# Early loads, interleaved attention pieces and an early w3 fetch in a retention-and-two-FFN kernel

## The chip, the core and the metric

The kernel runs on one core of one Trainium2 chip. The metric is the time on the device in microseconds (us); the median over several executions counts. One more execution was profiled: the trace has every instruction of the five engines, PE (TensorE matmul), DVE (VectorE), ACT (ScalarE), POOL (GpSimd) and SP (SyncE), and every DMA.

## The reference

Three stages follow each other: a decayed linear attention, a feed-forward layer with a piecewise quadratic activation, and a bilinear feed-forward layer with two output matrices.

```python
# attention: B, H, S, D = 4, 8, 768, 64
for t in range(S):
    state = gamma * state + k[:, :, t] (outer) v[:, :, t]
    y[:, :, t] = scale * q[:, :, t] @ state
x = y as (3072, 512)
# first layer: w_in (512, 2048), w_out (2048, 512)
h = x @ w_in
g = where(h >= 1, h, where(h <= -1, 0, (h + 1)**2 / 4))
x = g @ w_out
# second layer: w1, w2 (512, 1024), w3 (1024, 1024), w_out2 (1024, 512)
out = ((x @ w1) * (x @ w2) @ w3) @ w_out2
```

The weights arrive as 64-bit numbers and are turned into 32-bit floats on the chip.

## The kernel before, in words

The 3072 tokens are 6 tiles of 512. The attention runs over chunks of 128 tokens, so a tile is four chunks (g = 0 to 3 for the first). A chunk is three pieces (number a = 3g + part). Part 0 (L348, called qk here) multiplies the chunk's k and q into a PSUM tile `pa`; DVE multiplies that by the causal mask into `a_t` (L391). Part 1 (L358, called kv) multiplies k and v into `pa`; DVE makes `sbd` (chunk 0, L403) or `state` (L406) of it. Part 2 (L372, called out) multiplies the scaled q with `sbd` (not in chunk 0), then `a_t` with v, into `pa`; ACT copies it to `xh` (L412), DVE makes the next `sbd` of `state` (L415) and the remainder `xl` (L417). `piece_mm` issues a piece's matmuls, `piece_ew` what follows on ACT and DVE. `pa` has one buffer. Before the matmuls DVE or POOL multiplies q by `decay` (L315) and POOL scales v (L316).

For the first tile the loop is plainly: matmuls of piece a, loads and scaling for later chunks (`chunk_ahead`), elementwise work of piece a. q has two buffers, v and k one each. All loads are issued by SP, in the order of the code.

The conversion of weights is a generator of DVE steps (L184 to L215 or L231: five or six instructions on 512 or 1024 columns) that a small planner, `dve()`, fits into the gaps it expects on DVE. The first unit, win 0 and win 1 (the first two 128-column blocks of w_in), is converted one by one; then come pairs: wo 0 and 1 (of w_out), win 2 and 3, wo 2 and 3, and so on. A converted win block is split into a high part on ACT (L98) and a remainder on DVE (L99). The main loop then emits, for each step n, the matmuls `hps` of block f (L102 to L104: 12 matmuls, three per 128 rows), the activation `r` (L461 to L463) and the matmuls `y1acc` with w_out. Pieces of the later tiles lie between them.

All of w3, w1, w2 and w_out2 is converted in the same way during the first tiles and written to DRAM (`spill`). In the last tile (f = 0 to 15 counts its steps) w1 and w2 are fetched again and combined (`fetch_ab`, `prepare_ab`), and w_out2 is fetched and split (`load_wo2`). Then comes a stage that multiplies w3 by w_out2 (the w3 stage): 16 steps u, each with 12 matmuls of 128x512 into `w3acc`. Step u splits block u + 1 (`load_w3`, ACT then DVE) and then fetches block u + 2 into one of two buffers of tag f. The last two `prepare_ab`, the fetches of y (`fetch_y1`), their sums (`add_y`) and splits (`split_y`) and the evacuation of the product to `wc` lie in the same stage.

Of the kernel before, what the change touches and what calls it, by code (L numbers as in the profile page):

```python
# [37 lines left out]
PLAIN = 11  # L38
SINGLE = 1
# [10 lines left out]
def retention_then_two_ffns(  # L50
# [260 lines left out]
    def scale_chunk(g):  # L311
        if g >= NG:
# [4 lines left out]
            out=vp[g % 2],  # L317
# [16 lines left out]
    def piece_mm(a):  # L334
# [4 lines left out]
        q_t, kb, vb = ch[g], kp[g % 2], vp[g % 2]  # L339
        if part == 1 and c == NCH - 1:  # L340
            return
        ps = ps_a.tile([P, 2, 512], F32, tag="pa", name="pa")
        if part == 0:

            for p in range(NP):
                for h in range(2):
                    r = slice(64 * h, 64 * h + 64)
                    nc.tensor.matmul(  # L348
                        out=ps[:, h, p * C:(p + 1) * C], lhsT=kb[r, p, :], rhs=q_t[r, p, :],
                        start=True, stop=True,  # L350
                    )
            pe(1.0, ready[("q", g)])
        elif part == 1:

            for p in range(NP):
# [8 lines left out]
        else:  # L364


            for own in (False, True) if c else (True,):
                for j in range(NP // 2):
                    for h in range(2):
                        for e in range(2):  # L370
# [3 lines left out]
                                lhsT=vb[:, 2 * p + h, :] if own else sbd[r, p, :],  # L374
# [7 lines left out]
    def piece_ew(a):  # L382
# [6 lines left out]
        if part == 0:  # L389
            a_t = att.tile([P, 2, NP, C], F32, tag="a", name="a_t", bufs=1)  # L390
# [28 lines left out]
    def chunk_ahead(a):  # L419

        g, part = divmod(a, PIECES)
        if a < TILE_PIECES:
            if part == 0:
                if g:
                    load_qk(g + 1)
                scale_chunk(g + 1)
            elif part == 1:
                load_k(g + 1)
                load_v(g + 2)
        elif part == 0:  # L430
# [304 lines left out]
    with tc.manual_schedule():  # L735
# [14 lines left out]
        nc.sync.dma_start(out=decay, in_=c_decay)  # L750
        load_qk(0)
        load_v(0)
        nc.sync.dma_start(out=small, in_=c_small)
        scale_chunk(0)
        load_k(0)
# [4 lines left out]
        now["dma"] = 9.0  # L760
        load_job(jobs[0])
        load_v(1)


        early = [jobs[1]]
        for a in range(TILE_PIECES):
            piece_mm(a)
            chunk_ahead(a)
            if a == 2:
                load_job(early.pop(0))  # L770
            piece_ew(a)
# [4 lines left out]
        for n in range(-1, NA):  # L776
# [223 lines left out]
```

## Time and profile before

| what | value |
|---|---|
| median of 3 runs | 1108.78 us (1108.28 to 1109.03) |
| profiled execution, its own time | 1105.77 us |
| its span in the trace | 1104.0 us |
| PE busy | 1050.3 us, 95% of the span |
| DVE, ACT, POOL busy | 63%, 39%, 6% |

Engines run their own instructions in order and wait for each other by semaphores. PE is busy 95% of the span, so time can only come out of the other 5%, or out of matmuls that run at a lower clock: the granted clock of TensorE stands in a column of the stages, 1.00 for 2.4 GHz.

### The profile page before, as it was taken

What the parts mean: (1) busy time and instruction counts of PE and PEld (TensorE: products, weight loads), DVE (VectorE), ACT (ScalarE), POOL (GpSimd) and SP (SyncE); (2) the same over time, 40 slices, a digit from 0 to 9 for tenths busy, and PEclk for the clock granted to TensorE, in tenths of its full rate; (3) what the DMA queues carried; (4) which work ended last, traced back from release to release, by engine and by line L of the source; (5) the groups of instructions that cost most, each with busy time, mean ns of one, the idle gap of its engine ahead of it and who ended that gap; (6) DMA issues with size and microseconds to landing.
All of it is one profiled execution on the core that took longest, in us unless ns stands there. A gap on an engine that the chain in (4) does not pass through costs nothing.

```text
span 1104.0 us, 14147 instructions
## 1 busy us (share of the span) xinstructions
PE 1050.3 (95%) x5444; PEld 828.7 (75%) x5444; DVE 698.7 (63%) x1130; ACT 433.9 (39%) x763; POOL 71.5 (6%) x67
## 2 busy tenths in 40 slices
PE   4789999899999999999999998689999999999998
PEld 3555578677777777777788886478888888888886
DVE  4798888688888878877835774553445334623340
ACT  1223355344444445454435664432333223412220
POOL 2212000011110100000000010000000000000000
PEclk9789999999999999999999999899999999999999
DMA  6545225254443544354303665554544345523412
GB/s 208 181 154 181 77 96 183 85 172 173 164 152 124 170 136 153 124 173 142 115 2 132 248 239 196 185 200 172 187 166 143 131 176 172 189 105 134 167 34 77
DMA packets 64116, 166.03 MB, mean 150 GB/s; under 512 B 7600, under 2 KB 15920, under 8 KB 59312
## 3 DMA queue, kind: packets, MB, share of 16 engines
q1 hardware_dynamic: 61744, 150.44, 40.1%
q0 software_dynamic: 2304, 14.68, 3.7%
q8 instruction: 43, 0.70, 0.2%
q14 instruction: 25, 0.20, 0.1%
HBM read 125.24 MB, written 39.85 MB: 150 GB/s over the span
## 4 chain that ended last, share of the span: by engine, by line
PE 84%; DVE 6%; DMA 5%; ACT 2%; SPq 1%; issue 1%; POOL 1%; ACTq 0%; POOLq 0%; DVEq 0%
PE bank_a L673 12%; PE hps L103 8%; PE y1acc L102 8%; PE hps L102 8%; PE hps L104 8%; PE y1acc L103 7%; PE y1acc L104 7%; PE bank_b L673 6%; PE oacc L718 4%; PE oacc L720 4%; PE oacc L719 4%; PE bank_c L673 3%; PE pa L372 3%; DMA f<-sp_w 2%; PE y1acc L513 2%; PE pa L348 2%
## 5 line engine op out<-in xcount | busy, mean ns | idle before, releaser
L102 PE MATMUL hps<-xh,win 128*128 128x512 f32 x384 | 154.7, 403 | 6.3 <-ACT win L98 5.0
L103 PE MATMUL hps<-xh,win 128*128 128x512 f32 x384 | 151.7, 395 | 0.5 <-DVE win L99 0.5
L104 PE MATMUL hps<-xl,win 128*128 128x512 f32 x384 | 150.8, 393 | 0.4 <-DVE xl L417 0.4
L673 PE MATMUL bank_a<-yop,unit 128*128 128x512 f32 x576 | 145.7, 389 | 0.0
L102 PE MATMUL y1acc<-gh,wo_s 128*128 128x512 f32 x340 | 139.0, 409 | 4.9 <-ACT wo_s L98 4.9
L461 ACT ACTIVATE r<-hps 128x512 f32<-128x512 f32 x96 | 57.3, 597 | 218.3 <-PE hps L104 218.3
L103 PE MATMUL y1acc<-gh,wo_s 128*128 128x512 f32 x340 | 134.2, 395 | 0.5 <-DVE wo_s L99 0.5
L104 PE MATMUL y1acc<-gl,wo_s 128*128 128x512 f32 x340 | 133.6, 393 | 0.0
L463 DVE SCALAR_TENSOR_TENSOR r<-hps,r 128x512 f32<-128x512 f32 x96 | 66.3, 691 | 101.2 <-ACT r L462 100.7
L673 PEld LDWEIGHTS bank_a<-yop,unit 128*128 128x128 f32 x576 | 108.1, 188 | 22.5
L699 DVE TENSOR_TENSOR c<-bank_b,c 128x512 f32<-128x512 f32 x24 | 16.6, 692 | 131.5 <-PE bank_b L673 131.5
L102 PEld LDWEIGHTS hps<-xh,win 128*128 128x128 f32 x384 | 72.6, 189 | 25.2 <-ACT win L98 5.7
L103 PEld LDWEIGHTS hps<-xh,win 128*128 128x128 f32 x384 | 72.6, 189 | 18.6 <-DVE win L99 1.6
L104 PEld LDWEIGHTS hps<-xl,win 128*128 128x128 f32 x384 | 72.7, 189 | 17.0 <-DVE xl L417 1.3
L102 PEld LDWEIGHTS y1acc<-gh,wo_s 128*128 128x128 f32 x340 | 64.1, 189 | 23.7 <-ACT wo_s L98 5.7
L104 PEld LDWEIGHTS y1acc<-gl,wo_s 128*128 128x128 f32 x340 | 64.1, 189 | 14.5
L103 PEld LDWEIGHTS y1acc<-gh,wo_s 128*128 128x128 f32 x340 | 64.2, 189 | 13.9 <-DVE wo_s L99 1.6
L474 ACT CAST gh<-r 128x512 fp32r<-128x512 f32 x85 | 52.9, 622 | 52.6 <-DVE r L463 52.6
L673 PE MATMUL bank_b<-yop,unit 128*128 128x512 f32 x288 | 73.1, 389 | 0.0
L475 DVE TENSOR_TENSOR gl<-r,gh 128x512 fp32r<-128x512 f32 x85 | 60.6, 713 | 14.9 <-ACT gh L474 13.8
L99 DVE TENSOR_TENSOR wo_s<-wo_f,wo_s 128x512 fp32r<-128x512 f32 x85 | 61.9, 728 | 1.9 <-ACT wo_s L98 1.9
L315 POOL TENSOR_TENSOR q_t<-q_t,decay 128x512 f32<-128x512 f32 x23 | 32.6, 1416 | 465.4 <-DMA q_t<-in_qT_dram 438.0
(152 smaller groups left out, 1716.6 us busy)
## 6 DMA issues: line engine op xcount, KB each, us to landing
unit<-wab_d SPq DMA_DIRECT2D x24, 1024.0 KB, 4.8
unit<-wab_d SPq DMA_DIRECT2D x24, 768.0 KB, 4.3
raw<-in_w_in_dram SPq DMA_DIRECT2D x64, 128.0 KB, 3.0
raw<-in_w_dram SPq DMA_DIRECT2D x16, 512.0 KB, 4.0
raw<-in_w3t_dram SPq DMA_DIRECT2D x16, 512.0 KB, 3.8
wab_d<-four POOLq DMA_DIRECT2D x8, 1024.0 KB, 5.2
raw<-in_w_out_dram SPq DMA_DIRECT2D x14, 512.0 KB, 3.6
q_t<-in_qT_dram SPq DMA_DIRECT2D x24, 256.0 KB, 4.4
```

The lines of the kernel that those rows point to most:

```text
L99: nc.vector.tensor_tensor(out=lo, in0=src, in1=hi, op=ALU.subtract)
L102: nc.tensor.matmul(out=ps, lhsT=lh, rhs=rh, start=first, stop=False)
L103: nc.tensor.matmul(out=ps, lhsT=ll, rhs=rh, start=False, stop=False)
L104: nc.tensor.matmul(out=ps, lhsT=lh, rhs=rl, start=False, stop=last)
L461: nc.scalar.activation(out=r, in_=hps[n], func=AF.Relu, bias=0.5, scale=0.5)
L463: nc.vector.scalar_tensor_tensor(out=r, in0=hps.pop(n), scalar=1.0, in1=r, op0=ALU.max, op1=ALU.min)
L474: nc.scalar.copy(out=gh, in_=gs[n])
L475: nc.vector.tensor_tensor(out=gl, in0=gs[n], in1=gh, op=ALU.subtract)
L673: nc.tensor.matmul(out=ps, lhsT=x, rhs=z, start=first and kb + k == 0, stop=kb == 1 and k == 2, skip_group_check=True,)
L718: nc.tensor.matmul(out=ps, lhsT=lh, rhs=wh, start=(f == 0), stop=False)
L719: nc.tensor.matmul(out=ps, lhsT=lh, rhs=wl, start=False, stop=False)
L720: nc.tensor.matmul(out=ps, lhsT=ll, rhs=wh, start=False, stop=(f == NF2 - 1))
```

## The change

Five edits, in the parts that the diff shows. The first tile's four chunks get loads of their own, all issued at the start into buffers of the weight pool (`load_early`); POOL scales v in place. The constants and the loads of win 0 and win 1 are issued by ACT, not SP; each of the eight weight loads waits there until an earlier one of ACT's loads has landed. The pieces of the first tile run in a written order (`EARLY_ORDER`: number, 0 for matmuls and 1 for elementwise) with two `pa` buffers and, for part 1, the four buffers of `ps_acc`. The loads of chunk 4 and part of chunk 5 follow directly. `fetch_w3` loads w3 in pairs into the eight buffers that `wc` uses later, in steps f = 8 to 15 of the last tile.

```diff
+EARLY_ORDER = [(0, 0), (0, 1), (1, 0), (3, 0), (1, 1), (3, 1), (2, 0), (4, 0), (6, 0), (2, 1), (4, 1), (6, 1)]
+EARLY_ORDER += [(5, 0), (7, 0), (9, 0), (5, 1), (7, 1), (9, 1), (8, 0), (10, 0), (8, 1), (10, 1), (11, 0), (11, 1)]
...
-    ps_h = ctx.enter_context(tc.tile_pool(name="ps_h", bufs=2, space=bass.MemoryType.PSUM))
-    ps_a = tc.tile_pool(name="ps_a", bufs=1, space=bass.MemoryType.PSUM)
...
+    ps_a = early_psum.enter_context(
+        tc.tile_pool(name="ps_e", bufs=2, space=bass.MemoryType.PSUM)
+    )
...
+    first_keys = (("win", 0), ("win", 1))
...
+            queue = nc.scalar if key in first_keys else nc.sync
...
-        one = key[0] in ("wo2", "w3")
+        one = key[0] == "wo2"
...
+    def load_early():
+
+        for g in range(EARLY):
+            qk = wpool.tile([P, 2, 512], F32, tag="w", name="qk_e")
+            vk = wpool.tile([P, 2, 512], F32, tag="w", name="vk_e")
+            ch[g], kb[g] = (qk[:, i, :].rearrange("p (a t) -> p a t", a=NP) for i in range(2))
+            vt[g] = vb[g] = vk[:, 0, :].rearrange("p (h d) -> p h d", h=H)
+            kt[g] = vk[:, 1, :]
+            nc.sync.dma_start(out=ch[g], in_=qT[g])
+            nc.sync.dma_start(out=kb[g], in_=kT[g])
...
+            nc.sync.dma_start(out=vt[g], in_=v[g])
...
+            nc.sync.dma_start(out=kt[g], in_=k[g])
...
-        ps = ps_a.tile([P, 2, 512], F32, tag="pa", name="pa")
+        if g < EARLY and part == 1:
+            ps = ps_acc.tile([P, 1, 512], F32, tag="acc", name="pa")
+        else:
+            ps = ps_a.tile([P, 2, 512], F32, tag="pa", name="pa")
...
+            if g < EARLY:
+                a_t = wpool.tile([P, 2, 512], F32, tag="w", name="a_e")
...
+    def fetch_w3(u):
+
+        t = late.tile([P, 2, 512], F32, tag="wc", name="w3f", bufs=NF2)
+        for i in range(2):
+            nc.sync.dma_start(out=t[:, i, :], in_=spill[("w3", u + i)])
+            arrived[("w3", u + i)] = t[:, i, :]
...
+        nc.scalar.dma_start(out=decay, in_=c_decay)
+        nc.scalar.dma_start(out=small, in_=c_small)
         for h in range(2):
             r = slice(64 * h, 64 * h + 64)
-            nc.sync.dma_start(out=block[r], in_=c_block[r, :, 64 * h:64 * h + 64])
-        load_qk(1)
...
+            nc.scalar.dma_start(out=block[r], in_=c_block[r, :, 64 * h:64 * h + 64])
+        load_early()
         load_job(jobs[0])
...
+        load_job(jobs[1])
+        load_qk(EARLY)
+        load_v(EARLY)
+        load_k(EARLY)
+        for g in range(EARLY + 1):
+            scale_chunk(g)
+        load_v(EARLY + 1)
...
+        for a, ew in EARLY_ORDER:
+            (piece_ew if ew else piece_mm)(a)
+        early_psum.close()
...
-                    if j == NF2 - 1:
-                        fetch(("w3", 0), spill[("w3", 0)])
                 elif last:
                     load_wo2(NF2 - 1)
-                    fetch(("w3", 1), spill[("w3", 1)])
+                if f >= NF2:
+                    fetch_w3(2 * (f - NF2))
...
-            if u + 2 < 2 * NF2:
-                fetch(("w3", u + 2), spill[("w3", u + 2)])
```

PE, at the start of the program: before, the pieces of a chunk stand one behind the other (L348 is qk, L358 kv, L372 out).

```order
L348 MATMUL pa<-q_t,kp_90 128x128 x8
L358 MATMUL pa<-vp_92,k_t 64x64 x8
L372 MATMUL pa<-a_t,vp_92 64x128 x8
L348 MATMUL pa<-q_t,kp_91 128x128 x8
L358 MATMUL pa<-vp_93,k_t 64x64 x8
L372 MATMUL pa<-q_t,sbd 64x128 x8
L372 MATMUL pa<-a_t,vp_93 64x128 x8
L348 MATMUL pa<-q_t,kp_90 128x128 x8
```

After, qk of the next chunk and kv of this one stand ahead of each out piece (L380 is qk, L390 kv, L404 out; `qk_e` and `vk_e` are the new load buffers, `a_e` the masked product).

```order
L380 MATMUL pa<-qk_e 128x128 x8
L390 MATMUL pa<-vk_e 64x64 x8
L380 MATMUL pa<-qk_e 128x128 x8
L404 MATMUL pa<-a_e,vk_e 64x128 x8
L390 MATMUL pa<-vk_e 64x64 x8
L380 MATMUL pa<-qk_e 128x128 x8
L404 MATMUL pa<-qk_e,sbd 64x128 x8
L404 MATMUL pa<-a_e,vk_e 64x128 x8
```

The qk matmuls of chunk 1 moved ahead of the out matmuls of chunk 0, and those of chunk 2 ahead of the out matmuls of chunk 1.

DVE, in the same stretch, from the mask of chunk 1 on: before, the conversion of win 0 (`u`, `w_f`) begins behind the second `a_t`.

```order
L391 TENSOR_TENSOR a_t<-pa,small 128x1024
L184 TENSOR_SCALAR u<-u 128x512
L189 TENSOR_SCALAR u<-u 128x512
L194 SCALAR_TENSOR_TENSOR w_f<-raw,u 128x512
L406 TENSOR_TENSOR state<-pa,sbd 128x256
L199 TENSOR_SCALAR u<-w_f 128x512
L203 SCALAR_TENSOR_TENSOR u<-raw,u 128x512
L215 TENSOR_TENSOR w_f<-w_f,u 128x512
L415 TENSOR_TENSOR sbd<-state,block 128x256
L417 TENSOR_TENSOR xl<-pa,xh 128x4x128
```

After, the rows from the mask of chunk 3 (the last of the tile) to the `xl` of chunk 3.

```order
L427 TENSOR_TENSOR a_e<-pa,small 128x1024
L191 TENSOR_SCALAR u<-u 128x512
L196 TENSOR_SCALAR u<-u 128x512
L201 SCALAR_TENSOR_TENSOR w_f<-raw,u 128x512
L451 TENSOR_TENSOR sbd<-state,block 128x256
L453 TENSOR_TENSOR xl<-pa,xh 128x4x128
L442 TENSOR_TENSOR state<-pa,sbd 128x256
L206 TENSOR_SCALAR u<-w_f 128x512
L210 SCALAR_TENSOR_TENSOR u<-raw,u 128x512
L222 TENSOR_TENSOR w_f<-w_f,u 128x512
L451 TENSOR_TENSOR sbd<-state,block 128x256
L453 TENSOR_TENSOR xl<-pa,xh 128x4x128
```

All four masks now stand ahead of the first conversion instruction, so that when the tile's last `xl` is done (L453) only the conversion of win 0 is done, where before win 0, win 1 and four steps of wo 0 and 1 were.

SP, from the last tile into the w3 stage: before, the fetches of w3 (`sp_w_0` and on) begin around the writes of y (`y_d`) and then stand between the fetches of w1/w2 (`sp_wab`) and of y.

```order
L275 DMA f_5671<-sp_wo_6_2333 128x512
L275 DMA f_5748<-sp_wo_7_2386 128x512
L275 DMA f_5750<-sp_w_0_3634 128x512
L545 DMA y_d_86<-y1st 128x512 x4
L275 DMA f_5779<-sp_w_1_3696 128x512
L275 DMA f_5791<-sp_w_2_3755 128x512
L275 DMA f_5831<-sp_wab_3518 128x512
L275 DMA f_5833<-sp_wab_3569 128x512
L275 DMA f_5838<-sp_w_3_3812 128x512
L275 DMA f_5855<-sp_w_4_3920 128x512
L275 DMA f_5872<-sp_w_5_3987 128x512
```

After, they stand in pairs between the fetches of w_out2 (`sp_wo`) and w1/w2 of the last tile.

```order
L591 DMA w3f<-sp_w_0_3634 128x512
L591 DMA w3f<-sp_w_1_3696 128x512
L591 DMA w3f<-sp_w_2_3755 128x512
L591 DMA w3f<-sp_w_3_3812 128x512
L282 DMA f_5574<-sp_wo_5_2213 128x512
L282 DMA f_5576<-sp_wab_3349 128x512
L282 DMA f_5578<-sp_wab_3452 128x512
L591 DMA w3f<-sp_w_4_3920 128x512
L591 DMA w3f<-sp_w_5_3987 128x512
L591 DMA w3f<-sp_w_6_4039 128x512
L591 DMA w3f<-sp_w_7_4104 128x512
L282 DMA f_5683<-sp_wo_6_2333 128x512
```

The first w3 fetches moved from behind the last tile's last w_out2 fetch to ahead of the sixth, and their buffers (`w3f`) are not shared with it.

## Rows read from the trace of the kernel before

**Rows 1.** Waits of PE over the span: engine line, released by, us, times, longest

```profile
PE w3acc L102 <- ACT w3s L98: 10.9, 5, 5.0
PE pa L358 <- issue: 9.8, 5, 3.2
```

**Rows 2.** Stages: us, busy us by engine, PEclk, DMA share, GB/s

```profile
0.00:3.00 3.00, 0.00 (x0) 0.00 (x0) 0.00 (x0) 1.28 (x1) 0.20 (x4) 1.00 0.37 104
3.00:6.00 3.00, 0.81 (x8) 0.84 (x10) 0.69 (x1) 0.00 (x0) 0.00 (x0) 1.00 1.03 354
0.00:43.00 43.00, 22.07 (x241) 17.99 (x241) 21.97 (x34) 7.22 (x11) 10.03 (x13) 0.84 0.66 206
632.00:676.00 44.00, 41.45 (x182) 33.43 (x180) 30.91 (x63) 27.83 (x58) 3.19 (x6) 1.00 0.55 199
```

**Rows 3.** Timeline, first tile: start us, us, engine line operation [idle before <-releaser]

```profile
9.73 1.26 POOL L315 TENSOR_TENSOR q_t<-q_t,decay 128x512 f32<-128x512 f32 x1 [2.60 <-DMA q_t<-in_qT_dram]
...
13.70 2.08 PE L348 MATMUL pa<-q_t,kp 64*128 64x128 f32 x16 [1.46 <-issue]
15.82 1.23 DVE L391 TENSOR_TENSOR a_t<-pa,small 128x1024 f32<-128x1024 f32 x1 [2.22 <-PE pa L348]
16.96 0.42 DVE L184 TENSOR_SCALAR u<-u 128x512 f32<-128x512 f32 x1
...
18.48 0.42 DVE L406 TENSOR_TENSOR state<-pa,sbd 128x256 f32<-128x256 f32 x1
...
20.00 0.69 DVE L215 TENSOR_TENSOR w_f<-w_f,u 128x512 f32<-128x512 f32 x1
20.02 1.97 PE L372 MATMUL pa<-a_t,vp 128*64 128x128 f32 x16
...
22.66 0.69 DVE L417 TENSOR_TENSOR xl<-pa,xh 128x512 fp32r<-128x512 f32 x1 [1.63 <-ACT xh L412]
...
23.45 1.16 PE L348 MATMUL pa<-q_t,kp 64*128 64x128 f32 x16 [1.46 <-POOL vp L316]
...
42.98 0.50 PE L102 MATMUL hps<-xh,win 128*128 128x512 f32 x1 [0.69 <-ACT xh L412]
```

**Rows 4.** Timeline, DVE and PE where the main loop begins

```profile
58.13 1.29 DVE L99 TENSOR_TENSOR win<-w_f,win 128x512 fp32r<-128x512 f32 x2 [0.69 <-ACT win L98]
...
58.15 0.50 PE L102 MATMUL hps<-xh,win 128*128 128x512 f32 x1 [0.58 <-ACT win L98]
77.41 0.79 PE L102 MATMUL hps<-xh,win 128*128 128x512 f32 x1 [3.19 <-ACT win L98]
...
84.53 0.69 DVE L463 SCALAR_TENSOR_TENSOR r<-hps,r 128x512 f32<-128x512 f32 x1 [2.52 <-ACT r L462]
```

**Rows 5.** Tile w3acc: first and last start of its first line's matmuls

```profile
L102 PE MATMUL w3acc<-wo,w3s x64: 387/389/796, 676.0 to 739.0; 128*128 128x512 f32 x64
```

**Rows 6.** Timeline, PE in the w3 stage

```profile
704.93 0.80 PE L102 MATMUL w3acc<-wo,w3s 128*128 128x512 f32 x1 [5.04 <-ACT w3s L98]
...
710.52 0.63 PE L102 MATMUL w3acc<-wo,w3s 128*128 128x512 f32 x1
710.94 0.63 PE L103 MATMUL w3acc<-wo,w3s 128*128 128x512 f32 x1
...
711.88 0.40 PE L103 MATMUL w3acc<-wo,w3s 128*128 128x512 f32 x1
712.11 0.39 PE L104 MATMUL w3acc<-wo,w3s 128*128 128x512 f32 x1
```

**Rows 7.** Timeline, ACT and DVE in the w3 stage

```profile
704.26 0.62 ACT L98 CAST w3s<-f 128x512 fp32r<-128x512 f32 x1 [8.43 <-DMA f<-sp_w]
...
716.35 0.68 DVE L99 TENSOR_TENSOR w3s<-f,w3s 128x512 fp32r<-128x512 f32 x1
...
720.37 0.69 DVE L651 TENSOR_TENSOR t__6056<-f,f 128x512 f32<-128x512 f32 x1 [1.53 <-DMA f<-y_d]
...
722.31 0.68 DVE L99 TENSOR_TENSOR w3s<-f,w3s 128x512 fp32r<-128x512 f32 x1
```

More of the change, by code (lines that the diff above doesn't have):

```diff
@@ L72, in retention_then_two_ffns @@
     ps_acc = ctx.enter_context(tc.tile_pool(name="ps_acc", bufs=4, space=bass.MemoryType.PSUM))
-    ps_h = ctx.enter_context(tc.tile_pool(name="ps_h", bufs=2, space=bass.MemoryType.PSUM))
-    ps_a = tc.tile_pool(name="ps_a", bufs=1, space=bass.MemoryType.PSUM)
-    pairs_psum = ctx.enter_context(ExitStack())
-    ps_a = pairs_psum.enter_context(ps_a)
+    early_psum, pairs_psum = (ctx.enter_context(ExitStack()) for _ in range(2))
+    ps_a = early_psum.enter_context(
+        tc.tile_pool(name="ps_e", bufs=2, space=bass.MemoryType.PSUM)
+    )
+    ps_h = None
     dram = ctx.enter_context(tc.tile_pool(name="dram", bufs=1, space=bass.MemoryType.DRAM))
@@ L285, in retention_then_two_ffns @@
     at = {}
+    EARLY = TT // C
+    kb = {}
+    vb = {}
+    def load_early():
[7 more added lines that the diff above has]
+            nc.sync.dma_start(out=kb[g], in_=kT[g])
+            ready[("q", g)] = dma(256)
+            ready[("kT", g)] = dma(256)
+            nc.sync.dma_start(out=vt[g], in_=v[g])
+            ready[("v", g)] = dma(256)
+            nc.sync.dma_start(out=kt[g], in_=k[g])
+            ready[("k", g)] = dma(256)
     def load_qk(g):
@@ L289, in load_qk @@
             q_t = att.tile([P, NP, C], F32, tag="q", name="q_t")
-            kb = kp[g % 2]
+            kb[g] = kp[g % 2]
             nc.sync.dma_start(out=q_t, in_=qT[g])
-            nc.sync.dma_start(out=kb, in_=kT[g])
+            nc.sync.dma_start(out=kb[g], in_=kT[g])
             ch[g] = q_t
@@ L301, in load_v @@
             vt[g] = v_t
+            vb[g] = vp[g % 2]
             ready[("v", g)] = dma(256, now["pool"])
@@ L316, in scale_chunk @@
         nc.gpsimd.tensor_tensor(
-            out=vp[g % 2],
+            out=vb[g],
             in0=v_t,
@@ L348, in piece_mm @@
                     nc.tensor.matmul(
-                        out=ps[:, h, p * C:(p + 1) * C], lhsT=kb[r, p, :], rhs=q_t[r, p, :],
+                        out=ps[:, h, p * C:(p + 1) * C], lhsT=k_[r, p, :], rhs=q_t[r, p, :],
                         start=True, stop=True,
@@ L373, in piece_mm @@
                                 out=ps[64 * e:64 * e + 64, h, j * C:(j + 1) * C],
-                                lhsT=vb[:, 2 * p + h, :] if own else sbd[r, p, :],
+                                lhsT=v_[:, 2 * p + h, :] if own else sbd[r, p, :],
                                 rhs=at[g][:, h, p, :] if own else q_t[r, p, :],
@@ L389, in piece_ew @@
         if part == 0:
-            a_t = att.tile([P, 2, NP, C], F32, tag="a", name="a_t", bufs=1)
+            if g < EARLY:
+                a_t = wpool.tile([P, 2, 512], F32, tag="w", name="a_e")
+                a_t = a_t.rearrange("p h (a t) -> p h a t", a=NP)
+            else:
+                a_t = att.tile([P, 2, NP, C], F32, tag="a", name="a_t", bufs=1)
             nc.vector.tensor_tensor(
@@ L421, in chunk_ahead @@
         g, part = divmod(a, PIECES)
[L422 to L430, printed above, removed]
+        if part == 0:
             load_k(g)
@@ L748, in retention_then_two_ffns @@
                 (jobs if at_ < SINGLE else later).append(one)
[L750 to L755, printed above, removed]
+        nc.scalar.dma_start(out=decay, in_=c_decay)
+        nc.scalar.dma_start(out=small, in_=c_small)
         for h in range(2):
             r = slice(64 * h, 64 * h + 64)
-            nc.sync.dma_start(out=block[r], in_=c_block[r, :, 64 * h:64 * h + 64])
-        load_qk(1)
-        now["dma"] = 9.0
+            nc.scalar.dma_start(out=block[r], in_=c_block[r, :, 64 * h:64 * h + 64])
+        load_early()
         load_job(jobs[0])
[L762 to L771, printed above, removed]
+        load_job(jobs[1])
[8 more added lines that the diff above has]
+        early_psum.close()
+        ps_h = ctx.enter_context(tc.tile_pool(name="ps_h", bufs=2, space=bass.MemoryType.PSUM))
+        ps_a = pairs_psum.enter_context(
+            tc.tile_pool(name="ps_a", bufs=1, space=bass.MemoryType.PSUM)
+        )
         todo = deque(range(TILE_PIECES, NSTEP))
```

6 lines of the change are left out of this document (3 added, 3 removed).

## The prediction

> **What bounds the kernel now.** I looked first at who PE waits for over the whole span, because PE is busy 95% of it. Two waits lead [rows 1]: 10.9 us in the w3 stage, for the split of a w3 block on ACT, and 9.8 us in front of the kv pieces, where the trace names no engine (the one `pa` buffer has to be read first). They lie at the two ends that the change touches. The stages [rows 2] give the size of each. In the first 43 us PE is busy for 22.07 and DVE for 21.97: neither is the bound, they take turns. The first matmul of the main loop starts at 42.98 [rows 3]. The w3 stage, 676 to 740, is 192 matmuls long, and its waits and slow matmuls are taken apart below.
>
> Then I looked at what follows the first tile, since time won there must not be lost again. PE reaches win 2 at 58.15 and waits 0.58 us for it, reaches win 4 at 77.41 after 3.19 us of waiting [rows 4]. So from 43 to about 77 us the conversion on DVE is the bound, not PE. What the first tile gains counts only as far as DVE gets its conversions done earlier.
>
> **The first tile, step by step.** *Loads.* SP now issues 16 loads of 256 KB (4.19 MB), ACT the constants and win 0 and 1 (256 + 68 + 128 + 1024 KB, 1.51 MB). Before the change the DMA engines ran at a share of 1.03 and 354 GB/s from 3 to 6 us [rows 2], which is full. Up to 3 us they had moved 0.31 MB (3 us at 104 GB/s), 0.9 us of work at 354, so the first bytes flow at about 2.1 us. No row shows the short rows of win and block alone. Their cost lies between 354 GB/s and 206, the mean of the first tile [rows 2]; I take 206 for those 1.18 MB, since that is the only row that holds such loads, and 354 for the other 4.53 MB: 12.8 + 5.7 = 18.5 us, so the last load of chunk 3 lands at 20.6. All at 354 it would be 18.2; all at 206, 29.8.
>
> The rate of 354 came from SP alone. Weights issued by ACT therefore are not free, and I count them in the sum. The Trainium skill says the same in its page DMA: Bandwidth & Descriptors, section Issuing engines are not separate DMA queues: transfers of all issuers run on the same 16 engines, and a second issuer saves only the time to issue. By it the sum stays as it is; were the ACT loads free, chunk 3 would be there at 14.0 us, and the first tile would win 6.6 us more.
>
> *From chunk 3's loads to the main loop.* q of chunk 3 is issued three loads earlier, 2.2 us at 354, so it is there at 18.4, scaled by POOL at 19.7 (1.26), and qk is done at 20.9 (1.16 at the high clock). v lands one load ahead of k, at 19.9, and its scaling does not hold up qk. Then DVE runs a string in the new order [rows 3]: mask 1.23, three conversion steps 0.42 + 0.42 + 0.69, sbd 0.42, xl 0.69, state 0.42, three conversion steps 0.42 + 0.69 + 0.69, sbd 0.42, xl 0.69: 7.2 us, so 28.1. In between it waits for kv and two out pieces; such an out half took 1.97 us at the low clock. I add 2 us, the length of one of them: the main loop starts at **30** instead of 43. Were PE at the low clock all through (2.08 for a qk where 1.16 is the other level), it would be 5 us more. ACT issues twelve DMAs, the last eight each after an earlier one landed, ahead of its first copy (`xh` of chunk 0). As that copy is wanted after the second chunk's qk, I cost it at nothing; without that cover it holds up out of chunk 1 by some 2 us.
>
> *What DVE has not done by then.* In the new order DVE has done by that point one q (0.69), four masks (4.92), seven sbd or state (2.94), four xl (2.76) and six conversion steps (3.33): 14.6 us of work, against 21.97 [rows 2]. The missing 7.4 us, win 1 and the first steps of wo 0 and 1, come after. Before, win 2 came 15.2 us after the start of the loop (42.98 to 58.15); now 15.2 + 7.4 = 22.6 us after, at 52.6. So of 13 us 5.5 are left. PE then stands idle some 8 us more in that stretch, and comes back at a low clock: after the 3.19 us wait at 77.41 the first matmul took 0.79 and DVE then stood 2.52 us before the next r [rows 4]. I take 1.5 off (0 to 2.5). The first tile gives **4.0 us**. From win 2 on both orders are the same, and the waits at 77 us only move with DVE.
>
> **The w3 stage.** Its first line of matmuls starts at 676.0 and last at 739.0, with three pitches after it to the end [rows 5]: 63.7 us. A matmul at the high clock starts 0.23 us after the one before [rows 6], so 192 of them are 43.7 us. The excess is 20.0. Its largest wait, 5.04 us before 704.93 [rows 6], goes back to ACT standing 8.43 us until a w3 fetch landed [rows 7], and 14 matmuls behind it start 0.43 apart [rows 6], 2.9 us more. With w3 fetched from f = 8 on, no load of w3 is waited for, because the last pair is issued when the stage begins and is wanted 14 steps later. The buffers of `wc` are free then: step 7 evacuates into those of blocks 0 to 7, split by step 6.
>
> What stays: the start of the stage (0.5 us, and eight matmuls at the 0.43 pitch, 1.6 us), since nothing ahead of it moves. In steps 4 to 9 the splits stand on DVE behind `prepare_ab`, `add_y` and the evacuation; I allow 1.3 us in all. And one wait remains whole: `add_y` stands ahead of the split of block 10 and waits for a y load that is issued only when an earlier split frees its buffer. DVE's split of block 9 starts at 716.35, of block 10 at 722.31, with 1.53 us of waiting for y and four sums between [rows 7]; 6.0 us, for which PE has 12 matmuls, 2.7 us. 3.3 us remain, and with them perhaps 14 matmuls at the low clock, 0 to 2.9; I take 1.6. Sum 0.5 + 1.6 + 1.3 + 3.3 + 1.6 = 8.3, so the stage gives 20.0 - 8.3 = **11.7 us** (9 where DVE is later by 2.7, 14 where no low clock follows and the splits cost nothing).
>
> The fetches move 4.2 MB into the last tile. From 632 to 676 the DMA share was 0.55 at 199 GB/s [rows 2]; 4.2 MB in 44 us are 95 GB/s more, 294, below 354. I cost them at nothing.
>
> **Sum.** 4.0 + 11.7 = 15.7 us. The profiled execution took 1105.77 us (span 1104.0, 1.8 around it), so 1090.1. The median of the runs lies 3.0 us above it; on that scale it is 1093.
>
> **Rivals.** *DVE takes all of the first tile back.* If all loads run at 206 GB/s, chunk 3 is there at 29.8, the loop starts at 39 and win 2 comes at 61.8, 3.7 us later than before. With the w3 stage at its low end, 9 us, the gain is 5.3: 1103.5. For it speaks that the rate fell to 206 in the mean, against it that this mean contains stretches in which no load was asked for (share 0.66).
>
> *Both ends pay fully.* All loads at 354, or the weights of ACT free: loop start at 27, win 2 at 49.6, no clock loss, 8.5 us, and w3 14: 22.5, so 1086.3. For it speaks that PE is denser in the new order and may hold the high clock; against it the short rows of win.
>
> *The last tile starves (slower).* The w3 fetches stand on SP ahead of w1/w2 and w_out2 fetches. If DMA does not keep up, `prepare_ab` holds DVE, and with it the splits that PE needs next. It decides where each of the eight steps is 2.3 us later: 18 us, more than the gain. Against it: 294 GB/s wanted, 354 shown.
>
> *The change does not do what it says.* If PE in the w3 stage waited for buffers and not for loads, only 4 us are won: 1104.8. Against it ACT's releaser, a DMA [rows 7]. The first tile's pieces do interleave, by the order of PE.
>
> **How the numbers follow.** My forecast has 0.55 (1089 to 1101 by its own bounds: the first tile between -1.0 and 5.5, w3 between 9 and 14), both ends full 0.19, DVE takes it back 0.16, no effect on w3 0.05, starving 0.05. The range 1084 to 1104 holds the forecast, the full case and most of the third, and leaves out about 0.15. About 0.2% (2.2 us) is what a measurement of this kernel can tell from no change: faster 0.92 (all but starving and a corner of the third), same 0.04, slower 0.04.
>
> **What would show it.** In the new trace: the last load of chunk 3 near 20.6 us, the first `hps` matmul near 30, win 2 near 52.6 after a wait of PE for its split; a w3 stage near 52 us long, with no wait for a w3 fetch and one of about 3 us near its tenth step. I am wrong if the loop starts later than 35, if win 2 is not what PE waits for, or if a load of y or a clock at 1.2 GHz fills the w3 stage again.

## The result and the profile after

The changed kernel takes 1093.16 us in the median (1091.85 to 1093.40, 4 runs) against 1108.90 (1108.28 to 1109.59, 4 runs): a ratio of 0.9855, 95% interval 0.9838 to 0.9873, 15.7 us less. The profiled execution took 1093.40 us (span 1091.6), 12.4 us less than the profiled one of before; where the other 3.3 us are, the first experiment shows.

The timeline after, at the end of the first tile and in the main loop; it answers to [rows 3, 4].

```profile
20.37 1.26 POOL L344 TENSOR_TENSOR qk_e<-qk_e,decay 128x512 f32<-128x512 f32 x1 [1.72 <-DMA qk_e<-in_qT_dram]
22.74 1.04 POOL L345 TENSOR_TENSOR vk_e<-vk_e,small 128x512 f32<-128x512 f32 x1 [1.10 <-DMA vk_e<-in_v_dram]
22.90 1.23 DVE L427 TENSOR_TENSOR a_e<-pa,small 128x1024 f32<-128x1024 f32 x1 [1.84 <-PE pa L380]
24.07 1.52 POOL L344 TENSOR_TENSOR q_t<-q_t,decay 128x512 f32<-128x512 f32 x1 [0.29 <-DMA q_t<-in_qT_dram]
24.49 1.37 DVE L196 TENSOR_SCALAR u<-u 128x512 uint32<-128x512 uint32 x1
25.90 1.41 DVE L201 SCALAR_TENSOR_TENSOR w_f<-raw,u 128x512 uint32<-128x512 uint32 x1
27.24 0.41 DVE L451 TENSOR_TENSOR sbd<-state,block 128x256 f32<-128x256 f32 x1
...
31.78 0.76 PE L106 MATMUL hps<-xh,win 128*128 128x512 f32 x1 [1.50 <-DVE xl L453]
44.95 5.40 PE L541 MATMUL y1acc<-r,wo_f 128*128 128x512 f32 x8 [3.88 <-DVE wo_f L238]
55.16 0.50 PE L106 MATMUL hps<-xh,win 128*128 128x512 f32 x1 [3.19 <-ACT win L102]
```

The main loop starts at 31.78 instead of 42.98, 11.2 us earlier; win 2 comes at 55.16 instead of 58.15. The first tile still waits for loads: POOL stood 1.72 us for the q of chunk 3 and 1.10 us for its v. Between the last mask (22.90) and `sbd` two conversion steps take 1.37 and 1.41 us; the same two for the next block, at 32.60 and 33.06, take 0.43 and 0.69.

The stages after (us, busy us by engine, PEclk, DMA share, GB/s); they answer to [rows 2].

```profile
3.00:6.00 3.00, 0.96 (x8) 0.99 (x10) 0.69 (x1) 0.00 (x0) 0.00 (x0) 1.00 0.97 305
6.00:9.00 3.00, 2.13 (x28) 1.76 (x24) 1.23 (x1) 0.00 (x0) 1.04 (x1) 1.00 1.05 288
9.00:13.00 4.00, 2.34 (x21) 2.00 (x20) 0.53 (x2) 0.00 (x0) 2.30 (x2) 1.00 1.10 278
13.00:17.00 4.00, 2.62 (x38) 2.49 (x38) 1.47 (x2) 1.87 (x2) 1.26 (x1) 1.00 1.07 274
17.00:20.00 3.00, 2.84 (x62) 2.41 (x59) 2.23 (x4) 0.57 (x2) 1.04 (x1) 1.00 1.11 292
...
632.00:672.00 40.00, 37.78 (x164) 30.36 (x163) 26.93 (x55) 25.25 (x52) 3.19 (x6) 1.00 0.81 294
```

From 3 to 20 us the DMA engines are full (share about 1.0 to 1.1) and move 274 to 305 GB/s. The clock column needs care there: it reads 1.00 wherever the trace has no record of the clock, here up to 14.63 us (in [rows 2] up to 21.96). The same out matmuls of three chunks tell more:

```profile
12.78 1.97 PE L404 MATMUL pa<-a_e,vk_e 128*64 128x128 f32 x16
...
18.29 1.09 PE L404 MATMUL pa<-a_e,vk_e 128*64 128x128 f32 x16
...
28.30 1.97 PE L404 MATMUL pa<-a_e,vk_e 128*64 128x128 f32 x16
```

The second stands under a record of 2.4 GHz, the third under one of 1.2 GHz; by its length the first ran at 1.2 GHz too. In the last tile, with the fetches of w3, the DMA engines move 294 GB/s at a share of 0.81.

The tile `w3acc` after, which answers to [rows 5]:

```profile
L106 PE MATMUL w3acc<-wo,w3s x64: 387/389/632, 672.3 to 726.7; 128*128 128x512 f32 x64
```

The waits of PE over the span (us, times, longest), to [rows 1]:

```profile
PE w3acc L107 <- DVE w3s L103: 5.4, 5, 2.9
...
PE w3acc L106 <- ACT w3s L102: 1.7, 1, 1.7
```

And the timeline of the w3 stage, to [rows 6, 7]:

```profile
672.32 0.50 PE L106 MATMUL w3acc<-wo,w3s 128*128 128x512 f32 x1 [1.71 <-ACT w3s L102]
...
692.97 0.69 DVE L686 TENSOR_TENSOR t__5960<-f,f 128x512 f32<-128x512 f32 x1 [2.51 <-DMA f<-y_d]
...
696.26 0.50 PE L107 MATMUL w3acc<-wo,w3s 128*128 128x512 f32 x1 [1.65 <-DVE w3s L103]
...
705.58 0.69 DVE L686 TENSOR_TENSOR t__6058<-f,f 128x512 f32<-128x512 f32 x1 [1.57 <-DMA f<-y_d]
...
708.26 0.79 PE L107 MATMUL w3acc<-wo,w3s 128*128 128x512 f32 x1 [2.94 <-DVE w3s L103]
708.85 0.63 PE L108 MATMUL w3acc<-wo,w3s 128*128 128x512 f32 x1
709.28 0.63 PE L106 MATMUL w3acc<-wo,w3s 128*128 128x512 f32 x1
```

The stage is 55.0 us long (first to last of its 192 matmuls and one pitch), 63.8 before. No wait for a fetch of w3 is left. What is left is two waits, 1.65 and 2.94 us, behind DVE's sums, which wait for y loads, and 22 matmuls that start more than 0.36 us after the one before, at 1.2 GHz, 9 at the stage's start and 13 behind the second wait. Counted from 0, the two waits lie in steps 7 and 10.

### The profile page after: what moved, and what is told of

It reads as the page before. It is cut to its first block, busy times and chain, and to the rows that moved or that the text cites. A ratio compares the mean times of both kernels' runs of the same rounds, so it can differ in the third digit from the quotient of the medians.

```text
span 1091.6 us, 14117 instructions
## 1 busy us (share of the span) xinstructions
PE 1047.6 (96%) x5444; PEld 828.7 (76%) x5444; DVE 700.1 (64%) x1130; ACT 434.0 (40%) x763; POOL 70.3 (6%) x67
## 4 chain that ended last, share of the span: by engine, by line
PE 87%; DVE 6%; DMA 3%; ACT 2%; issue 1%; POOL 0%; DVEq 0%; ACTq 0%; SPq 0%
PE bank_a L708 12%; PE hps L107 8%; PE hps L106 8%; PE hps L108 8%; PE y1acc L106 8%; PE y1acc L107 7%; PE y1acc L108 7%; PE bank_b L708 6%; PE oacc L753 4%; PE oacc L755 4%; PE oacc L754 4%; PE bank_c L708 3%; PE pa L404 3%; PE y1acc L541 2%; PE pa L380 2%; DMA raw<-in_w_in_dram 1%
## 5 line engine op out<-in xcount | busy, mean ns | idle before, releaser
L503 DVE TENSOR_TENSOR gl<-r,gh 128x512 fp32r<-128x512 f32 x85 | 60.1, 707 | 14.9 <-ACT gh L502 13.8
L708 PEld LDWEIGHTS bank_b<-yop,unit 128*128 128x128 f32 x288 | 54.1, 188 | 11.2
```

Of the source, the lines that this page charges most:

```text
L503: nc.vector.tensor_tensor(out=gl, in0=gs[n], in1=gh, op=ALU.subtract)
L708: nc.tensor.matmul(out=ps, lhsT=x, rhs=z, start=first and kb + k == 0, stop=kb == 1 and k == 2, skip_group_check=True,)
```

## The experiments

Unless another base is named, each is the changed kernel with one edit. "Stage" is the w3 stage as counted above, "half-clock" the number of its matmuls that start 0.36 to 0.47 us after the one before, where 0.23 is the pitch at 2.4 GHz.

| kernel | median us (range, runs) | ratio to before, 95% | win 2 at | w3 stage from, long | half-clock |
|---|---|---|---|---|---|
| before again | 1108.33 (1105.1-1110.57, 10) | 0.9993 (0.998-1.0006) | 60.30 | 679.9, 63.1 | 18 |
| w3 only | 1097.29 (1096.53-1099.4, 4) | 0.9902 (0.9881-0.9924) | 59.93 | 679.3, 52.0 | 8 |
| first tile only | 1103.98 (1101.2-1108.0, 10) | 0.9964 (0.9947-0.9982) | 54.55 | 670.9, 63.8 | 20 |
| weights behind | 1088.03 (1087.7-1089.1, 4) | 0.9817 (0.9794-0.9841) | 51.17 | 668.3, 53.4 | 14 |
| weights between | 1092.04 (1091.6-1094.74, 4) | 0.9851 (0.9832-0.987) | 57.17 | 674.4, 53.8 | 17 |
| two issuers | 1089.01 (1088.02-1090.16, 4) | 0.9825 (0.9805-0.9845) | 51.94 | 670.0, 51.9 | 6 |
| POOL late | 1093.01 (1092.27-1093.71, 4) | 0.9861 (0.9845-0.9878) | 55.84 | 673.2, 53.3 | 14 |
| conversion early | 1092.66 (1088.37-1093.0, 4) | 0.9849 (0.9825-0.9873) | 55.69 | 673.7, 53.2 | 13 |
| y early | 1090.69 (1086.66-1092.47, 4) | 0.9835 (0.981-0.9861) | 57.24 | 676.2, 49.0 | 0 |
| y order | 1090.38 (1089.9-1091.31, 4) | 0.9835 (0.9818-0.9852) | 57.27 | 674.7, 50.6 | 8 |
| both | 1084.25 (1083.29-1086.47, 4) | 0.9781 (0.9762-0.9801) | 51.45 | 668.8, 48.9 | 8 |
| both, sums later | 1083.19 (1080.95-1086.2, 4) | 0.9771 (0.9747-0.9795) | 50.64 | 669.6, 47.5 | 0 |

The rows were measured in three groups, each beside executions of before: the first four rows (before's median 1108.57 us), "weights between", "POOL late", "conversion early" and "y early" (1107.70), the others (1108.70). The changed kernel's 1093.16 stood beside 1108.90. Medians of different groups can therefore differ by about 1 us without a cause in the kernel; the ratios take such a shift out.

### The kernel before, once more

No edit.

> The kernel before, unchanged, profiled once more. The two profiled executions differ by 12.4 us (1105.77 and 1093.40), the two medians by 15.7. Theory A: the profiled execution of before was a lucky one, and a typical one loses about 3 us more at a place that hangs on a DMA, so I expect 1108 to 1109 us here, with the first tile (start of the main loop at 43) and win 2 (58.2) as they were, and the 3 us in the w3 stage (about 66 to 67 us long instead of 63.7). Rival B: the 3 us lie in the first tile, so that its gain in the median is 6.6 and not 3.6. Rival C: they are spread over the main loop as a clock a little lower, and neither term changes.

The profiled execution took 1108.94 us, 3.2 us more than the first one. The timeline of PE:

```profile
15.05 2.08 PE L348 MATMUL pa<-q_t,kp 64*128 64x128 f32 x16 [1.46 <-POOL vp L316]
...
24.86 2.08 PE L348 MATMUL pa<-q_t,kp 64*128 64x128 f32 x16 [1.53 <-POOL vp L316]
...
44.40 0.80 PE L102 MATMUL hps<-xh,win 128*128 128x512 f32 x1 [0.69 <-ACT xh L412]
...
60.30 0.49 PE L102 MATMUL hps<-xh,win 128*128 128x512 f32 x1 [0.57 <-ACT win L98]
...
225.80 0.62 PE L103 MATMUL y1acc<-gh,wo_s 128*128 128x512 f32 x1 [0.22 <-DVE wo_s L99]
226.22 0.63 PE L104 MATMUL y1acc<-gl,wo_s 128*128 128x512 f32 x1
```

Theory A is wrong, B and C each have a part. All of the first tile is 1.35 us later from the first load on (15.05 against 13.70 in [rows 3]), the qk of chunk 2 takes 2.08 us where it took 1.16, and win 2 comes 2.15 us later. Another 1.6 us are eight matmuls at 1.2 GHz from 225.80 on, which the first trace did not have. The w3 stage is no longer than before (63.1 against 63.8). The median of several executions is therefore the fair scale.

### Each half of the change alone

The kernel before with the edits for w3 alone (in part; the other hunks are those of the change):

```diff
-        one = key[0] in ("wo2", "w3")
+        one = key[0] == "wo2"
...
-                    fetch(("w3", 1), spill[("w3", 1)])
+                if f >= NF2:
+                    fetch_w3(2 * (f - NF2))
```

> Before, with the fetches of w3 alone changed (in pairs, from step f = 8 of the last tile on, into the buffers of the conversion); the first tile as it was. Theory A (the two halves of the change add up, and this one is the larger): the w3 stage is 55 us long as in the changed kernel, 8.6 us less than the 63.7 of before's trace, and the median 9 to 12 us below before: 1097 to 1100. Rival B (the first tile carries the median): 4 to 7 us below, 1102 to 1105.

And the changed kernel with the same edits undone:

> The changed kernel with its w3 fetches put back as before, so that the first tile alone is changed. Theory A: main loop from 31.8 us, win 2 at 55.2, w3 stage begun about 3.6 us earlier than before and as long as before: 3 to 4.5 us below before, 1104.5 to 1106. Rival B: 6 to 7 us below, 1102. Rival C (a denser first tile is taken back wholly by the conversion): within 1 us of before.

The w3 edit alone gives 10.9 us by its ratio (8.4 to 13.2 by the interval), the first tile alone 4.0 (2.0 to 5.9); together 14.9, measured together 16.1 (14.1 to 18.0) by the ratio. The halves add up, theory A (the median of the first tile alone lies 0.5 us below its range); the runs of the first tile alone scatter by 6.8 us, so its interval is wide. Which of the first tile's edits (early loads, written order, PSUM buffers) wins how much was not tried. The w3 stage of the first kernel is 52.0 us long, 3 us less than in the changed kernel, with the same code and the same waits. The timeline of its second long wait:

```profile
713.49 0.64 PE L103 MATMUL w3acc<-wo,w3s 128*128 128x512 f32 x1 [2.85 <-DVE w3s L99]
```

The waits are 5.3 us here and 5.4 in the changed kernel, but only 8 matmuls run slowly, not 22: 14 x 0.2 us = 2.8. Seven of the kernels have this stage unchanged; their stages are 51.9 to 55.0 us long, in the mean 53.2, with 5.2 to 5.4 us of waits and 6 to 22 slow matmuls.

### Who issues the weights, and behind what

```diff
-    first_keys = (("win", 0), ("win", 1))
+    first_keys = ()
```

With this, SP issues win 0 and 1 behind the 16 loads of the chunks ("weights behind").

> The changed kernel with win 0 and win 1 issued by SP, behind the 16 loads of the chunks, instead of by ACT beside them. Theory A (all transfers share the same rate, about 280 GB/s here, so ACT's issue only sets the order): the chunks land 1.0 MB / 280 GB/s = 3.7 us earlier, the last kv piece no longer waits, the main loop starts 2 to 3 us earlier, near 29, but the first conversion steps come later by as much, DVE waits for them, and win 2 stays within 1.5 us of 55.2: the median within 1.5 us of the changed kernel. Rival B (ACT's issues are a gain of their own, a second path): the last load lands no earlier, win 2 comes 3 us or more later, and the time is 2 to 3 us worse, 1095.5. Rival C (transfers of the chunks are what the first tile waits for): 2 to 3 us better, 1090.5.

With the same line and the next edit, SP issues win 0 behind chunk 0 and win 1 behind chunk 1 ("weights between").

```diff
             nc.sync.dma_start(out=kt[g], in_=k[g])
             ready[("k", g)] = dma(256)
+            if g < 2:
+                mark = now["dma"]
+                load_job(jobs[g])
+                now["dma"] = mark
```

(`mark` keeps the planner's times, and with them the order on DVE and PE, as they were.)

> The changed kernel with the same loads in about the same order of bytes, but all issued by SP: win 0 behind chunk 0, win 1 behind chunk 1, no weights on ACT; DVE's and PE's order unchanged. It tells order from issuer, after weights behind all chunks on SP gave 1088.0 where weights on ACT gave 1093.2. Theory A (the bytes ahead of chunk 3 decide, whoever issues them): the last mask of the first tile at 22 to 24 us on DVE (22.9 in the changed kernel, 18.9 with the weights behind), main loop near 31.5, median 1092 to 1095. Rival B (ACT's issuing is itself the cost, by its own queue or by the table load and xh behind it): close to the weights-behind kernel, 1088 to 1089.5.

And "weights behind" with half of the chunks' loads on ACT:

```diff
-            nc.sync.dma_start(out=vt[g], in_=v[g])
+            nc.scalar.dma_start(out=vt[g], in_=v[g])
...
-            nc.sync.dma_start(out=kt[g], in_=k[g])
+            nc.scalar.dma_start(out=kt[g], in_=k[g])
```

> Weights behind the chunks on SP, and of the chunks v and k issued by ACT instead of SP. It asks whether a second issuer helps by itself, when it doesn't bring other bytes forward. Theory A (all transfers share one rate, at a DMA share of 1.0 between 9 and 17 us): the last mask within 0.7 us of 18.9, median 1087.5 to 1088.7. Rival B (SP's issue, 0.43 us each and one wait after the other, holds the loads up): last mask 1.5 us or more earlier, 1086.5 or less. Rival C (ACT's issues hold up its xh): main loop later, 1089 to 1090.

Weights behind the chunks, the stages and the timeline of the last mask, the loop's start and win 2:

```profile
9.00:13.00 4.00, 3.10 (x26) 2.88 (x28) 1.25 (x2) 0.00 (x0) 3.15 (x3) 1.00 1.04 364
13.00:17.00 4.00, 4.00 (x73) 3.64 (x70) 2.57 (x5) 0.58 (x1) 2.63 (x3) 1.00 1.09 344
```

```profile
18.88 1.22 DVE L427 TENSOR_TENSOR a_e<-pa,small 128x1024 f32<-128x1024 f32 x1
...
27.60 0.76 PE L106 MATMUL hps<-xh,win 128*128 128x512 f32 x1 [2.86 <-DVE xl L453]
...
51.17 0.51 PE L106 MATMUL hps<-xh,win 128*128 128x512 f32 x1 [3.19 <-ACT win L102]
```

The chunks alone come at 344 to 364 GB/s where the mixture came at 274 to 278. Every milestone is 4.0 to 4.2 us earlier than in the changed kernel (22.90, 31.78, 55.16), and the median 5.1 us lower (4.2 by the ratios): rival C, and more than it asked for. My theory A failed in one point: DVE's conversion hardly waits for the later weights (0.88 us), because they come while DVE is still at the masks.

Weights between the chunks, the timeline of DVE and PE:

```profile
25.74 1.22 DVE L431 TENSOR_TENSOR a_e<-pa,small 128x1024 f32<-128x1024 f32 x1 [0.30 <-PE pa L384]
...
27.33 0.43 DVE L196 TENSOR_SCALAR u<-u 128x512 uint32<-128x512 uint32 x1
27.79 0.69 DVE L201 SCALAR_TENSOR_TENSOR w_f<-raw,u 128x512 uint32<-128x512 uint32 x1
...
32.62 0.47 PE L106 MATMUL hps<-xh,win 128*128 128x512 f32 x1 [2.05 <-DVE xl L457]
```

No weights on ACT, and still nothing is won over the changed kernel beyond the spread: 1092.0, the last mask at 25.7 (I expected 22 to 24; now all the weights stand ahead of chunk 2). So it is the bytes ahead of chunk 3 that cost, not the issuer. Two issuers for the chunks bring no gain either: the last mask at 19.41 against 18.88, the median 1089.0 against 1088.0; theory A by the mask, 0.3 us above its range by the time; the main loop is not later (27.37 against 27.60), so it is not rival C either. The Trainium skill's page DMA: Bandwidth & Descriptors, section Issuing engines are not separate DMA queues, says that transfers of all issuers run on the same engines; both kernels agree.

### POOL beside DVE

```diff
-        for g in range(EARLY + 1):
+        for g in range(EARLY):
             scale_chunk(g)
-        load_v(EARLY + 1)
...
             (piece_ew if ew else piece_mm)(a)
+        scale_chunk(EARLY)
+        load_v(EARLY + 1)
```

> The changed kernel with POOL's scaling of chunk 4 (two operations, 1.52 and 1.22 us) put behind the first tile's pieces in the program. Theory A (two conversion steps of DVE took 1.37 and 1.41 us instead of 0.43 and 0.69 because POOL worked beside them): these two steps are back at 0.43 to 0.7, the main loop starts 1.0 to 1.7 us earlier, near 30.3, and the median is 0.5 to 1.7 us lower, 1091.5 to 1092.7. Rival B (POOL's semaphore order puts the scaling at the same time as before, since POOL waits only for the load): no change, the two steps still slow, 1093. Rival C (the scaling then comes too late for chunk 4): a new wait of PE before chunk 4's qk, 1 us or more later, 1094.

The timeline of POOL and DVE:

```profile
24.72 1.52 POOL L344 TENSOR_TENSOR q_t<-q_t,decay 128x512 f32<-128x512 f32 x1 [0.28 <-DMA q_t<-in_qT_dram]
25.15 1.38 DVE L196 TENSOR_SCALAR u<-u 128x512 uint32<-128x512 uint32 x1
...
26.20 1.23 POOL L345 TENSOR_TENSOR vp<-v_t,small 128x512 f32<-128x512 f32 x1
26.56 1.41 DVE L201 SCALAR_TENSOR_TENSOR w_f<-raw,u 128x512 uint32<-128x512 uint32 x1
```

Rival B: POOL waits only for the load, so its place in the program's text moves nothing, and the edit did not test its theory. "Weights between" did, unasked. There POOL was done at 25.65:

```profile
24.61 1.04 POOL L349 TENSOR_TENSOR vp<-v_t,small 128x512 f32<-128x512 f32 x1 [0.59 <-DMA v_t<-in_v_dram]
```

The same two steps, behind it, took 0.43 and 0.69 (above). From the last mask to the main loop it took 6.9 us, in the changed kernel 8.9.

### The conversion earlier

```diff
         load_job(jobs[0])
         load_job(jobs[1])
+        now["dma"] = mark
+        ready[("raw", jobs[0][2])] = 13.0
+        ready[("raw", jobs[1][2])] = 18.0
```

(`mark` is the planner's DMA time ahead of the two loads; its rate in the first tile is set from 350 to 270.)

> The changed kernel with the planner told that the weights are there at 13 and 18 us, so that DVE does win 0's conversion between the masks of the first tile, and one step of win 1, instead of behind them; same work. It tests the step of the prediction by which the conversion undone at the loop's start comes back in full at win 2. Theory A: DVE stood idle for some 10 us before its last mask (22.9), and about 3 us of conversion more fit there; the two waits of PE in the first 25 us of the loop (3.88 us before y1acc at 44.95 and 3.19 us for win 2 at 55.16) shrink by as much, win 2 at 51 to 53, median 1089.5 to 1091.5. Rival B (a conversion step ahead of a mask holds up the pieces behind it): the loop starts later by what the steps take and win 2 does not move: 1093 to 1094.

The timeline of DVE and PE in the main loop:

```profile
37.16 0.69 DVE L491 SCALAR_TENSOR_TENSOR r<-hps,r 128x512 f32<-128x512 f32 x1 [3.69 <-ACT r L490]
...
40.28 0.50 PE L106 MATMUL hps<-xh,win 128*128 128x512 f32 x1 [3.36 <-ACT win L102]
...
55.69 0.80 PE L106 MATMUL hps<-xh,win 128*128 128x512 f32 x1 [4.06 <-ACT win L102]
```

A miss, and not by the way of rival B. Only three of win 0's six steps went ahead of the last mask. The loop did start a little earlier (31.27), but the planner now put `r` of block 0 ahead of the last steps of win 1's conversion; DVE stood 3.69 us for `r` with that work behind it, and PE waited 3.36 us for win 1 instead of 3.88 for wo. Win 2 did not move. Whether an order without this stand would gain was not tried, so the step of the prediction stays argued, not tested.

### The y loads in the w3 stage

```diff
-        ahead = y_of(0)
+        ahead = [(0, kb, name) for kb in range(2) for name in ("p1", "p2", "p3", "p6", "p5", "p7", "p4")]
...
-            elif u == 3:
+            elif u == 2:
                 prepare_ab(EARLY_AB + 1)
```

> The changed kernel with the last prepare_ab of the w3 stage one step earlier (u = 2, not 3) and the splits of the first y tile's blocks ordered so that the y buffers come free earlier. It tests what holds the w3 stage at 55.1 us. Theory A (a y load is issued only when a buffer comes free, DVE stands 2.51 and 1.57 us for it, and PE then 1.65 and 2.94 us for the w3 split behind it, with 13 matmuls at half clock after the second): these waits fall to under 1 us in all, the stage is 51 to 52.5 us long, the median 3 to 4.5 us lower, 1088.5 to 1090. Rival B (DVE is simply full there: prepare_ab, add_y and four splits, so that the wait moves to another split): the stage stays within 1 us of 55, 1092 to 1094.

The first of the two hunks alone:

> The changed kernel with only the order of the splits of the first y tile changed (p1, p2, p3, then the sums), prepare_ab left at u = 3. It takes the two waits of the w3 stage apart, after both edits together made the stage 49.0 us long (55.1 in the changed kernel) and removed the waits at steps 5 and 9 but put one of 1.75 us before step 4. Theory A (each wait has its own y load: the first hangs on prepare_ab, the second on the splits): DVE's wait for the first y load stays at about 2.5 us and PE's at 1.65, the second, 2.94 us, falls to 1.3 or less, the half clock behind it goes; stage 51 to 53 us, median 1.5 to 3 us below the changed kernel, 1090 to 1091.5. Rival B (the second wait is DVE's own work): stage unchanged, 1093.

The timeline of "y order":

```profile
695.38 0.69 DVE L686 TENSOR_TENSOR t__5960<-f,f 128x512 f32<-128x512 f32 x1 [2.53 <-DMA f<-y_d]
...
698.65 0.50 PE L107 MATMUL w3acc<-wo,w3s 128*128 128x512 f32 x1 [1.68 <-DVE w3s L103]
...
709.00 0.50 PE L107 MATMUL w3acc<-wo,w3s 128*128 128x512 f32 x1 [1.32 <-DVE w3s L103]
```

Theory A held for the order of the splits: DVE no longer waits for the second y load, PE's wait fell from 2.94 to 1.32 us, and no matmul behind it is slow; the stage is 50.6 us long and the median 2.8 us lower (2.2 by the ratios). (The waits that the expectation puts in steps 5 and 9 are those of steps 7 and 10.) The earlier `prepare_ab` only traded: it removed the 1.68 us, and put 1.75 us before step 4, where the split now stands behind it (waits 3.9 us against 3.8). The trace of "y early" shows why it is no better there:

```profile
685.74 0.72 ACT L102 CAST four<-f 128x256 fp32r<-128x256 f32 x2 [2.50 <-DMA wab_d<-four]
...
689.71 0.50 PE L106 MATMUL w3acc<-wo,w3s 128*128 128x512 f32 x1 [1.75 <-ACT w3s L102]
```

ACT stands 2.50 us until the result of the `prepare_ab` before has been written out of the same buffer (`four`). I had expected at least 3.6 us less of waits from both edits; 1.5 came, all of it from the order, and the medians of the two kernels are 0.3 us apart. "Y early" missed its ranges: its stage is shorter than expected (49.0 us) and its median 0.7 us too high at the same time, because in its trace the stage starts at 676.2, 3.9 us later than in the changed kernel's, with the same code ahead of it. What makes that difference is open.

### Together

"Both" is "weights behind" with the two edits of "y early".

> Weights behind the chunks on SP together with the earlier prepare_ab and the new order of splits. Theory A (two ends, separate causes, the gains add): 1088.0 - 2.3 = 1085.7, with win 2 near 51 and a w3 stage near 49 to 50.5 us; range 1084 to 1087. Rival B (what the first tile gains is lost again at the w3 stage): 1088.

"Both, sums later" has one edit more:

```diff
             load_w3(u + 1)
+            if u == NF2 + 1:
+                add_y(0, 1)
             emit_w3o(u)
...
-            if u == NF2:
-                add_y(0, 1)
```

> The kernel of both, with add_y of the second half one step later (in step 9, behind the split for step 10), so that the sums no longer stand ahead of that split. Theory A (DVE's order alone makes PE wait 1.32 us there): this wait is below 0.4 us and nothing behind it is later, 1.0 us below the kernel of both. Rival B (the wait moves to step 11 or 12, since the sums have to be done anyway): within 0.5 us of the kernel of both.

The tile `w3acc` of the last one:

```profile
L106 PE MATMUL w3acc<-wo,w3s x64: 388/389/503, 669.5 to 716.4; 128*128 128x512 f32 x64
```

Theory A in both: the gains at the two ends add (1084.25, expected 1084 to 1087), and with the sums behind the split the 1.3 us wait is gone (47.5 us for the stage). The last kernel has a wait of 1.78 us before step 4 that "both" has not, but that is not a loss: in "both" eight matmuls at the stage's start ran at 1.2 GHz, and step 4 begins 13.5 us after the stage's start in either. The last kernel takes 1083.19 us, 25.5 less than before and 10.0 less than the changed kernel (9.3 by the ratios); its 1.1 us over "both" lie inside the spread of the four runs of each.

## Why the prediction was right, and where its steps were off

The forecast of 1093 us was met to 0.2 us, with the mechanism of the likeliest case; both halves came near their terms (4.0 predicted and 4.0 measured alone; 11.7 predicted, 10.9 measured alone). So close a hit is partly luck, for some of its steps were off and made up for each other.

**The scale.** I set the sum against the profiled execution's own time and then added 3.0 us for the median. On the own scale I was wrong by 3.3 us (1090.1 against 1093.4). On the median's scale the sum was right, because the profiled execution of before was a quick one in the first tile and in the main loop, as its second trace shows, not at the w3 stage.

**Loads.** Predicted: v of chunk 3 at 19.9 us, with 354 GB/s for the chunks and 206 for the weights' rows; it came at 22.7. The order of size was right, the sum of the two rates too quick: the mixture ran at 274 to 305 from 3 to 20 us. That ACT's weights count was right; I did not draw the consequence that they need not stand ahead of the chunks at all, which is worth another 4 to 5 us.

**From the loads to the loop.** Predicted 7.2 us of DVE work and 2 us of waiting behind qk, loop at 30; measured 31.78, from a mask that was 2.0 us late. The string took longer by some 1.7 us, not for the waits but for the two conversion steps beside POOL, and the 2 us allowed covered that. ACT's issues cost nothing: its first `xh` came late, at 16.04, but DVE's next mask had to wait for qk until 17.8 anyway.

**What DVE has not done.** Predicted 22.6 us from the loop's start to win 2, measured 23.4, and 23.4 to 25.1 in the other kernels with this order. The step held by its number: of 11.2 us won in the first tile 3.0 were left at win 2 (5.1 against the second trace of before), and 3.6 at the stage's start (7.5). Of the 7.5 us 1.6 are the half-clock stretch at 226 us of that trace, which the change does not touch. DVE is busy for 19.9 of the 23.4 us, which speaks for the reason given; the one experiment on it missed. The 1.5 us taken off for a low clock do not show as a loss of their own: from win 2 to the w3 stage the changed kernel takes 617.2 us, the two traces of before 617.8 and 619.6. The 4.0 us measured alone, with its interval of 2.0 to 5.9, cannot tell 4.0 from the 5.5 without that term.

**The w3 stage.** Predicted 52 us, the trace has 55.0, the seven traces with this code 53.2 in the mean. No fetch is waited for, as said. The wait near the tenth step was put at 3.3 us and is 2.9. What I missed is another, 1.65 us in step 7, of the same kind: the y loads for the first half stand behind `prepare_ab`. For the splits on DVE I had allowed 1.3. The half clock was put at 3.2 us (1.6 at the start, 1.6 behind the wait); it is 1.2 to 4.4 in the seven traces, for no cause that they show. Of the 11.3 us that the stage after takes beyond 192 pitches, 4.6 are the two waits behind y loads and 4.4 the half clock, where the prediction had 3.3 and 3.2 of 8.3; what it named as a sign of being wrong, a y load or 1.2 GHz in this stage, came in part.

**The fetches.** Forecast 294 GB/s in the last tile, measured 294, at a share of 0.81, and nothing waits for it.

**The rivals.** "DVE takes all back" and "starves" are out by the 4.0 us and the DMA share, "the change does not do what it says" by the 10.9 us of the w3 edit alone. "Both ends full" is what "weights behind" does at the first tile: win 2 at 51.2, near the 49.6 of that rival, and 1088.0 us in all, where it had 1086.3.

## What to carry to other kernels

When loads are issued early, ask what each byte stands ahead of: 1 MB of weights beside the first chunks cost 4 to 5 us, issued by ACT or by SP, and behind them only a wait of 0.88 us. A wait that is removed uncovers the next one on the same engine's queue; list all loads whose buffer comes free only by work in that queue, not just the one that you see. Compare medians of executions, or several traces, before you explain 3 us out of two single traces.

## What was unexpected in the hardware

DVE slows beside POOL: two conversion steps that take 0.43 and 0.69 us took 1.37 and 1.41 while POOL multiplied from and to SBUF, and POOL's own 1.26 became 1.52; masks that read PSUM, beside POOL too, kept their 1.23. The Trainium skill has it in its page SBUF — State Buffer, section SBUF: two separate sides: DVE and GpSimd share a pair of ports, and a DVE instruction in a two-port mode, or with two SBUF inputs beside a GpSimd instruction that reads SBUF, and the GpSimd instruction lock each other out for the whole instruction, whoever starts first. The traces agree, with each slow step ending 0.3 to 0.6 us after POOL's; the 1.41 us step has two SBUF inputs (`raw`, `u`), the 1.37 us one has one, and its mode stands in no trace. It costs some 1.7 us of the first tile here.

Of the same code with the same waits the clock makes different times: after the wait of 2.8 to 2.9 us in the w3 stage 6 to 13 matmuls ran at 1.2 GHz, and at the stage's start none, eight or nine, from one execution to the next, 0.2 us each.
